# Decay scans that read PSUM and restart by a maximum, in an RWKV-6 plus mixture-of-depths kernel

## The chip, the cores and the metric

The kernel runs on one core of a Trainium2 chip. The metric is the device time of one execution in microseconds (us); the lower, the better. The engines of the core are TensorE (PE, with its weight loads PEld), VectorE (DVE), ScalarE (ACT), GpSimd (POOL) and SyncE (SP), which here only issues DMAs. PE writes its results to PSUM, and the other memory that the engines read is SBUF.

## What is computed

The first block is a linear attention with a decay per channel, over batch B = 4, heads H = 8, sequence S = 768 and head size D = 48:

```python
for t in range(S):
    cur = einsum('bhd,bhe->bhde', u * k_t, v_t)
    y[:, :, t] = einsum('bhd,bhde->bhe', r_t, state + cur)
    state = w_t[..., None] * state + einsum('bhd,bhe->bhde', k_t, v_t)
```

The second block takes y as rows of 384 = H * D numbers. It scores each row with a vector, picks the 128 best rows of each batch, sends them through a two-layer MLP (384 to 1024, ReLU, back to 384) and adds the result, gated by a sigmoid of the score, to these rows. All is float32. The decays w lie between 0.8 and 0.95.

## The kernel before, in words

**Tiling.** The sequence of a batch is cut into 6 chunks of L = 128 steps, 24 chunks in all. Two heads are one pair, each head padded to 64 channels, so a pair fills 128 partitions; HP = 4 pairs lie side by side, 128 steps each (W = 512 columns).

**Work on a chunk.** `decays` (lines 203 to 236) transposes the chunk's decays on PE (line 200, four transposes into one PSUM buffer `ps_t`), copies them with ACT into the SBUF buffer `wz` with a zero column between two pairs (line 208), and makes two running products with DVE scans over all four pairs at once. `right` (line 211) runs backward and holds, for each step, the product of the decays behind it. A scan step is state = data0 * state + data1; the zero column clears the state and `from_right` adds a 1 there, so each pair begins anew. The full product of a chunk, `all`, is a column of `right`; its reciprocal (line 218) is the start value, in `from_left`, of the forward scan `left` (line 223). Two ACT activations then check that the decays are in range (line 232). `scaled` (line 238) transposes k and r on PE and multiplies them by `right` and `left` (line 244, DVE): tiles K and R. `own` (line 247) makes the term with u, two products and one more on POOL (lines 251, 252, 256) with a DVE sum between (line 254), and issues the loads of a later chunk on SP. `scores` (line 260) multiplies K by R on PE and masks the result on DVE (line 271, `sc`). `back` (line 274) transposes K on PE, and ACT copies it out of PSUM (line 277, `kt`). `outputs` (line 282) sums the state part (line 289) and the chunk's own part (line 295) on PE; DVE adds (line 300, `x`) and scores the rows (line 302). `carry` (line 309) brings the state on: PE (line 319), DVE (lines 327 or 330), POOL (line 328, times the next chunk's `all`), ACT (line 334, into `s_buf`).

**Buffers.** The transposes of w, k, r and K share one pool of three PSUM buffers (`psT`, line 93, tag "t"). A buffer is given back when the last reader of its tile has ended.

**Order.** The loop from line 491 writes the pieces in this order for chunk n: scores(n), own(n+1), scaled(n+1), back(n), outputs(n), decays(n+2), carry(n), with one step of the previous batch's `mixture` between two pieces. The order on each engine is set when the program is built: a list scheduler goes by this order as priority and by its own estimates of when an instruction is ready, and so lets a later piece's instruction fill the time in which an earlier one waits. On the chip each engine then runs its list in order. After the last chunk `mixture` of the last batch runs by itself.

Of the kernel before, what the change touches and what calls it, by code (L numbers as in the profile page):

```python
# [10 lines left out]
FP32 = mybir.dt.float32  # L11
# [4 lines left out]
ALU = mybir.AluOpType  # L16
AX = mybir.AxisListType

L = 128
# [18 lines left out]
def kernel(  # L38
# [28 lines left out]

    nc = tc.nc  # L70
    PSUM = bass.MemoryType.PSUM

    B, H, S, D = r.shape
# [4 lines left out]
    HP = H // 2  # L78
# [1 line left out]
    NFC = F // L  # L80
    NHF = NCH // 2
    W = HP * L
    LS = L + 1
    WS = HP * LS
    assert S % (2 * L) == 0 and C % L == 0 and F % (4 * L) == 0 and H % 2 == 0
    assert D <= DP and W <= 512 and C <= 512 and 0 < CAP < S and CAP % L != 1
    assert B * NCH < 256
# [82 lines left out]
    nc.vector.tensor_copy(out=ids, in_=number)  # L170


    from_right = consts.tile([L, WS], FP32)
    nc.any.memset(from_right, 0.0)
    nc.vector.memset(from_right.rearrange("p (j t) -> p j t", t=LS)[:, :, 0], 1.0)
    from_left = [consts.tile([L, WS], FP32, name=f"from_left{i}") for i in range(2)]
    for t in from_left:
        nc.any.memset(t, 0.0)

    wz_bufs = [consts.tile([L, WS + 1], FP32, name=f"wz_buf{i}") for i in range(2)]  # L180
    for t in wz_bufs:
        nc.any.memset(t, 0.0)

    s_bufs = [consts.tile([L, HP, 2, D], FP32, name=f"s_buf{i}") for i in range(2)]
    for t in s_bufs:
# [2 lines left out]
    views = dram_disjoint_views(out, B)  # L188
    score = consts.tile([L, B, NCH], FP32)
    guard = consts.tile([L, N, 2], FP32)  # L190

    def by_pair(ap, at):

        return ap[:, at:at + WS].rearrange("p (j t) -> p j t", t=LS)[:, :, 0:L]


    def transposed(src, j=None):
# [5 lines left out]
    def decays(t):  # L203
        n = t["n"]
        wb = w_bufs[n % NBUF]
        ps = transposed(lambda j: wb[:, 2 * j:2 * j + 2, :])
        wz = wz_bufs[n % len(wz_bufs)]
        nc.scalar.copy(out=by_pair(wz, 1), in_=ps)  # L208
        yield
        right = lev.tile([L, WS + 4], FP32, tag="right", name="right", bufs=3)  # L210
        nc.vector.tensor_tensor_scan(  # L211
            out=right[:, WS:0:-1], data0=wz[:, WS:0:-1], data1=from_right, initial=0.0,
            op0=ALU.mult, op1=ALU.add,
        )
        t["right"] = right
        t["all"] = right[:, 1:1 + WS].rearrange("p (j t) -> p j t", t=LS)[:, :, 0]
        start = from_left[n % len(from_left)]
        nc.vector.reciprocal(  # L218
            out=start.rearrange("p (j t) -> p j t", t=LS)[:, :, 0], in_=t["all"]
        )  # L220
        yield
        left = lev.tile([L, WS], FP32, tag="left", name="left")
        nc.vector.tensor_tensor_scan(  # L223
            out=left, data0=wz[:, 0:WS], data1=start, initial=0.0,
            op0=ALU.mult, op1=ALU.add,
        )
        t["left"] = left
        yield

        junk = lev.tile([L, H, D], FP32, tag="junk", name="junk")  # L230
        for i, (bias, scale) in enumerate(((low, -1.0), (high, 1.0))):
            nc.scalar.activation(
                out=junk, in_=wb[:, :, 0:D], func=AF.Relu, bias=bias, scale=scale,
                accum_out=guard[:, n, i:i + 1],
            )
        yield

    def scaled(t):
        n = t["n"]
        rb, kb = r_bufs[n % NBUF], k_bufs[n % NBUF]  # L240
        for name, src, by in (("K", kb, by_pair(t["right"], 2)), ("R", rb, by_pair(t["left"], 0))):
            ps = transposed(lambda j: src[:, 2 * j:2 * j + 2, :])
            t[name] = lev.tile([L, HP, L], FP32, tag=name, name=name)
            nc.vector.tensor_mul(t[name], ps, by)  # L244
            yield
# [94 lines left out]
    def mixture(b):  # L340
# [38 lines left out]
        for gi, (c0, n) in enumerate(groups):  # L379

            pick = mod.tile([L, NCH, L], BF16, name="pick")
            at = rank
# [8 lines left out]
            for c in range(NCH):  # L391
# [2 lines left out]
                )  # L394
            idx = mod.tile([L, 1], UINT32, name="idx", bufs=2)
            nc.vector.tensor_scalar(
                out=idx, in0=ps[:, 0:1], scalar1=ps[:, 1:2], scalar2=None, op0=ALU.add
            )
            rows = views[b][0:b + 1].rearrange("b s c -> (b s) c")
            where = bass.IndirectOffsetOnAxis(ap=idx[0:n, 0:1], axis=0)  # L400
# [188 lines left out]
```

## Time and profile before

| what | value |
|---|---|
| time, median of 3 runs | 338.93 us (337.67 to 341.52) |
| the profiled execution's own time | 339.1 us |
| its span in the profile | 337.3 us |
| busy: PE, DVE, POOL, ACT | 272.4, 207.9, 111.6, 85.5 us |
| mean granted PE clock | 0.77 of full speed |
| instructions | 5344 |

The span runs from the first to the last instruction that the profile shows; 1.8 us of the execution's time lie around it. Busy times of different engines overlap, so they are not added up. A line number is that of the kernel before.

### The profile page before, as it was taken

How to read it: one execution, taken by the hardware profiler on the slowest of the kernel's cores; microseconds unless marked ns; L12 is line 12 of the kernel's file. 1: busy time of each engine (PE TensorE's matmuls, PEld its weight loads, DVE VectorE, ACT ScalarE, POOL GpSimd, SP SyncE). 2: the span in 40 equal slices, each digit the busy share in tenths (PEclk: the TensorE clock that was granted, in tenths of full speed). 3: DMA queues.
4: the chain of work that ended last, by engine and by line, in shares of the span. 5: the costliest groups of instructions: out<-in, count | busy, mean ns of one | idle time of the engine just before them, and what ended most of it. 6: DMA issues, size and time to landing. Idle time of an engine off the chain costs nothing.

```text
span 337.3 us, 5344 instructions
## 1 busy us (share of the span) xinstructions
PE 272.4 (81%) x2034; PEld 239.5 (71%) x2034; DVE 207.9 (62%) x411; ACT 85.5 (25%) x209; POOL 111.6 (33%) x108
## 2 busy tenths in 40 slices
PE   0148797997979899979869899979879899992691
PEld 0037796996967798769768699678867699681570
DVE  6139777677986854785976753866986723737100
ACT  1143334143431412331520402332411103120010
POOL 2154446364700664254600343264600200010001
PEclk9999859587875569995965559996965559995597
DMA  7999767355867811462633501464400000010001
GB/s 251 258 200 172 126 117 119 77 98 84 139 98 122 113 48 36 107 141 69 133 57 72 117 23 25 93 151 87 96 2 23 23 25 0 25 48 23 26 0 33
DMA packets 105570, 29.14 MB, mean 86 GB/s; under 512 B 100416, under 2 KB 104768, under 8 KB 105536
## 3 DMA queue, kind: packets, MB, share of 16 engines
q1 hardware_dynamic: 103584, 23.99, 40.4%
q10 hardware_dynamic: 1440, 3.15, 2.6%
q0 software_dynamic: 512, 1.57, 1.6%
q8 instruction: 18, 0.29, 0.4%
q14 instruction: 16, 0.13, 0.2%
HBM read 23.20 MB, written 5.51 MB: 85 GB/s over the span
## 4 chain that ended last, share of the span: by engine, by line
PE 58%; DVE 17%; DMA 7%; issue 7%; SPq 5%; POOL 3%; ACT 1%; POOLq 0%; DVEq 0%; ACTq 0%
PE ps_y L295 15%; PE ps_h L444 9%; PE ps_t L200 9%; PE ps_y L289 7%; PE ps_s L265 6%; PE ps_f L455 6%; DVE left L223 4%; DVE right L211 4%; PE ps_kv L319 3%; DMA xe<-out_dram,idx 3%; DMA r_buf<-in_r_dram 2%; DVE ahead L361 2%; DVE scr L302 2%; SPq L121 2%; DVE sc L271 1%
## 5 line engine op out<-in xcount | busy, mean ns | idle before, releaser
L295 PE MATMUL ps_y<-v,sc 128*128 128x48 f32 x384 | 71.0, 318 | 7.6 <-DVE sc L271 7.6
L295 PEld LDWEIGHTS ps_y<-v,sc 128*128 128x128 f32 x384 | 67.7, 248 | 9.2 <-DVE sc L271 8.7
L289 PE MATMUL ps_y<-s_buf,R 128*128 128x96 f32 x160 | 42.5, 357 | 10.4 <-ACT s_buf L334 10.4
L300 DVE TENSOR_TENSOR x<-ps_y,vo 128x384 f32<-128x384 f32 x24 | 13.4, 558 | 60.3 <-PE ps_y L295 60.3
L256 POOL TENSOR_TENSOR vo<-v,own 128x384 f32<-128x384 f32 x24 | 26.5, 1106 | 71.6 <-DVE x L300 36.2
L265 PE MATMUL ps_s<-R,K 48*128 48x128 f32 x384 | 42.4, 354 | 0.0
L289 PEld LDWEIGHTS ps_y<-s_buf,R 128*128 128x128 f32 x160 | 32.3, 250 | 11.8 <-ACT s_buf L334 11.8
L211 DVE TENSOR_TENSOR_SCAN right<-wz_buf,from_right 128x516 f32<-128x516 f32 x24 | 36.9, 1536 | 5.9 <-ACT wz_buf L208 5.9
L265 PEld LDWEIGHTS ps_s<-R,K 48*128 48x128 f32 x384 | 34.2, 242 | 5.9 <-issue 3.0
L200 PE MATMUL ps_t<-ident,w_buf 128*128 128x128 f32 x96 | 21.0, 354 | 19.5 <-DMA w_buf<-in_w_dram 16.2
L251 POOL TENSOR_TENSOR rk<-r_buf,k_buf 128x384 f32<-128x384 f32 x24 | 29.5, 1231 | 20.0 <-DMA r_buf<-in_r_dram 20.0
L252 POOL TENSOR_TENSOR rk<-rk,u_bc 128x384 f32<-128x384 f32 x24 | 34.0, 1421 | 1.8 <-DMA u_bc<-in_u_dram 0.5
L328 POOL TENSOR_TENSOR state<-mid,right 128x192 f32<-128x192 f32 x16 | 12.2, 763 | 66.1 <-DVE from_left L218 41.1
L444 PE MATMUL ps_h<-xeT,w 128*128 128x128 f32 x192 | 32.5, 346 | 0.6 <-ACT xeT L414 0.6
L223 DVE TENSOR_TENSOR_SCAN left<-wz_buf,from_left 128x516 f32<-128x516 f32 x24 | 32.3, 1345 | 0.2
L444 PEld LDWEIGHTS ps_h<-xeT,w 128*128 128x128 f32 x192 | 31.4, 259 | 1.3 <-ACT xeT L414 1.0
L271 DVE TENSOR_TENSOR sc<-ps_s,before_f 128x512 f32<-128x512 f32 x48 | 30.9, 675 | 1.7 <-PE ps_s L265 1.5
L200 PEld LDWEIGHTS ps_t<-ident,w_buf 128*128 128x128 f32 x96 | 15.5, 198 | 21.6 <-issue 16.5
L208 ACT COPY wz_buf<-ps_t 128x512 f32<-128x512 f32 x24 | 14.1, 585 | 59.3 <-PE ps_t L200 58.8
L277 ACT COPY kt<-ps_t 128x512 f32<-128x512 f32 x24 | 13.9, 581 | 50.3 <-PE ps_t L200 50.1
L200 PE MATMUL ps_t<-ident,r_buf 128*128 128x128 f32 x96 | 20.8, 355 | 6.6 <-DVE K L244 6.6
L334 ACT COPY s_buf<-state 64x192 f32<-64x192 f32 x40 | 14.0, 350 | 40.0 <-POOL state L328 34.7
(83 smaller groups left out, 352.6 us busy)
## 6 DMA issues: line engine op xcount, KB each, us to landing
w_buf<-in_w_dram SPq DMA_DIRECT2D x24, 192.0 KB, 3.2
k_buf<-in_k_dram SPq DMA_DIRECT2D x24, 192.0 KB, 4.0
r_buf<-in_r_dram SPq DMA_DIRECT2D x24, 192.0 KB, 4.5
v<-in_v_dram SPq DMA_DIRECT2D x24, 192.0 KB, 3.5
out_dram<-x SPq DMA_DIRECT2D x24, 192.0 KB, 2.0
w<-in_moe_w_dram ACTq DMA_DIRECT2D x2, 1536.0 KB, 9.8
u_bc<-in_u_dram SPq DMA_DIRECT2D x1, 192.0 KB, 4.3
wg_bc<-in_moe_w_gate_dram SPq DMA_DIRECT2D x1, 192.0 KB
```

What stands on the lines that cost most here:

```text
L200: nc.tensor.transpose(ps[:, j, :], src(j), ident)
L211: nc.vector.tensor_tensor_scan(out=right[:, WS:0:-1], data0=wz[:, WS:0:-1], data1=from_right, initial=0.0, op0=ALU.mult, op1=ALU.add,)
L223: nc.vector.tensor_tensor_scan(out=left, data0=wz[:, 0:WS], data1=start, initial=0.0, op0=ALU.mult, op1=ALU.add,)
L251: nc.gpsimd.tensor_mul(rk, rb[:, :, 0:D], kb[:, :, 0:D])
L252: nc.gpsimd.tensor_mul(rk, rk, u_bc)
L256: nc.gpsimd.tensor_mul(t["vo"], values[n], o.to_broadcast([L, H, D]))
L265: nc.tensor.matmul(ps[:, par, j, :], t["K"][rows, j, :], t["R"][rows, j, :], start=True, stop=True,)
L271: nc.vector.tensor_mul(t["sc"][:, par], ps[:, par], _heads(before_f, HP))
L289: nc.tensor.matmul(y[:, 2 * j:2 * j + 2, :], t["R"][:, j, :], s_bufs[n % len(s_bufs)][:, j], start=True, stop=False,)
L295: nc.tensor.matmul(y[:, h, :], t["sc"][:, par, j, :], vt[:, h, :], start=(ci == 0), stop=(ci == 0 or par == 1),)
L444: nc.tensor.matmul(ps[:, q, :], w1[:, dc, (f0 + q) * L:(f0 + q + 1) * L], xeT[:, dc, :], start=(dc == 0), stop=(dc == NDC - 1),)
L455: nc.tensor.matmul(ps, hid[:, fc, :], w2[:, fc, :], start=(fc == 0), stop=(fc == NFC - 1))
```

## The change

The ACT copy to `wz` and the zero columns go. Both scans read the transposed decays where PE left them, in PSUM, 511 columns instead of 516. The restart between two pairs is made by a maximum in place of the sum: a step is now state = max(data0 * state, data1), with data1 zero but at a pair's first step, where it holds 1 (backward) or the reciprocal of `all` (forward); the product that runs on from the pair before is never above these. `right` is written so that the last column of the last pair is a constant 1, set once in three fixed buffers. `all` is now its own tile of 128x4, a DVE product of a column of PSUM and a column of `right`. The first column of `left` is copied by ACT, one element per partition, since the forward scan writes from the second column on. K and R read `right` and `left` without gaps. In `mixture`, the sum that makes the row index takes a maximum with the batch's first row in the same instruction.

```diff
-    from_right = consts.tile([L, WS], FP32)
+    from_right = consts.tile([L, HP, L], FP32)
...
-    wz_bufs = [consts.tile([L, WS + 1], FP32, name=f"wz_buf{i}") for i in range(2)]
-    for t in wz_bufs:
-        nc.any.memset(t, 0.0)
+    right_bufs = [consts.tile([L, HP, L], FP32, name=f"right_buf{i}") for i in range(3)]
+    for t in right_bufs:
+        nc.vector.memset(t[:, HP - 1, L - 1:L], 1.0)
...
         ps = transposed(lambda j: wb[:, 2 * j:2 * j + 2, :])
-        wz = wz_bufs[n % len(wz_bufs)]
-        nc.scalar.copy(out=by_pair(wz, 1), in_=ps)
-        yield
-        right = lev.tile([L, WS + 4], FP32, tag="right", name="right", bufs=3)
+        wt = ps.rearrange("p j t -> p (j t)")
+
+        right = t["right"] = right_bufs[n % len(right_bufs)]
+        flat = right.rearrange("p j t -> p (j t)")
         nc.vector.tensor_tensor_scan(
-            out=right[:, WS:0:-1], data0=wz[:, WS:0:-1], data1=from_right, initial=0.0,
-            op0=ALU.mult, op1=ALU.add,
+            out=flat[:, W - 2::-1], data0=wt[:, W - 1:0:-1],
+            data1=from_right.rearrange("p j t -> p (j t)")[:, W - 2::-1], initial=1.0,
+            op0=ALU.mult, op1=ALU.max,
         )
-        t["right"] = right
-        t["all"] = right[:, 1:1 + WS].rearrange("p (j t) -> p j t", t=LS)[:, :, 0]
+        t["all"] = lev.tile([L, HP], FP32, tag="all", name="all", bufs=3)
+        nc.vector.tensor_mul(t["all"], ps[:, :, 0], right[:, :, 0])
         start = from_left[n % len(from_left)]
-        nc.vector.reciprocal(
-            out=start.rearrange("p (j t) -> p j t", t=LS)[:, :, 0], in_=t["all"]
+        nc.vector.reciprocal(out=start[:, :, 0], in_=t["all"])
+        yield
+
+        left = t["left"] = lev.tile([L, HP, L], FP32, tag="left", name="left")
+        nc.scalar.copy(out=left[:, 0, 0:1], in_=start[:, 0, 0:1])
+        nc.vector.tensor_tensor_scan(
+            out=left.rearrange("p j t -> p (j t)")[:, 1:W], data0=wt[:, 0:W - 1],
+            data1=start.rearrange("p j t -> p (j t)")[:, 1:W], initial=start[:, 0, 0:1],
+            op0=ALU.mult, op1=ALU.max,
         )
-        yield
-        left = lev.tile([L, WS], FP32, tag="left", name="left")
-        nc.vector.tensor_tensor_scan(
-            out=left, data0=wz[:, 0:WS], data1=start, initial=0.0,
-            op0=ALU.mult, op1=ALU.add,
-        )
-        t["left"] = left
...
             nc.vector.tensor_scalar(
-                out=idx, in0=ps[:, 0:1], scalar1=ps[:, 1:2], scalar2=None, op0=ALU.add
+                out=idx, in0=ps[:, 0:1], scalar1=ps[:, 1:2], scalar2=float(b * S),
+                op0=ALU.add, op1=ALU.max,
             )
```

## Rows read from the trace of the kernel before

**Rows 1.** Page: busy time by engine; granted PE clock in 40 slices.

```profile
PE 272.4 (81%) x2034; PEld 239.5 (71%) x2034; DVE 207.9 (62%) x411; ACT 85.5 (25%) x209; POOL 111.6 (33%) x108
...
PEclk9999859587875569995965559996965559995597
```

**Rows 2.** Windows of 2 us: width, busy per engine, PEclk, DMA share, GB/s.

```profile
76.00:78.00 2.00, 0.01 (x1) 0.00 (x0) 2.00 (x3) 1.18 (x3) 1.92 (x2) 1.00 1.44 185
...
80.00:82.00 2.00, 2.00 (x11) 2.00 (x11) 0.31 (x1) 0.00 (x0) 0.00 (x0) 0.50 0.00 0
```

**Rows 3.** Chain that ended last, shares of the span by line.

```profile
PE ps_y L295 15%; PE ps_h L444 9%; PE ps_t L200 9%; PE ps_y L289 7%; PE ps_s L265 6%; PE ps_f L455 6%; DVE left L223 4%; DVE right L211 4%; PE ps_kv L319 3%; DMA xe<-out_dram,idx 3%; DMA r_buf<-in_r_dram 2%; DVE ahead L361 2%; DVE scr L302 2%; SPq L121 2%; DVE sc L271 1%
```

**Rows 4.** The same chain in order of time: start, us, what.

```profile
22.61 1.45 DVE left L223
24.06 1.71 DVE right L211
...
242.48 1.94 DVE right L211
...
246.24 1.14 DVE left L223
```

**Rows 5.** Single lines' instructions: duration ns min/median/max, first and last start.

```profile
L211 DVE TENSOR_TENSOR_SCAN right<-wz_buf,from_right x24: 1220/1429/2243, 10.8 to 286.7; 128x516 f32<-128x516 f32 x24
...
L223 DVE TENSOR_TENSOR_SCAN left<-wz_buf,from_left x24: 1214/1223/1850, 22.5 to 288.2; 128x516 f32<-128x516 f32 x24
...
L271 DVE TENSOR_TENSOR sc<-ps_s,before_f x48: 656/680/692, 30.3 to 299.5; 128x512 f32<-128x512 f32 x48
...
L252 POOL TENSOR_TENSOR rk<-rk,u_bc x24: 993/1402/1922, 21.0 to 243.4; 128x384 f32<-128x384 f32 x24
...
L300 DVE TENSOR_TENSOR x<-ps_y,vo x24: 556/558/558, 34.7 to 303.3; 128x384 f32<-128x384 f32 x24
...
L302 DVE CUSTOM_DVE_ANT_0 scr<-x,wg_bc x24: 534/556/1353, 35.7 to 303.9; 128x384 f32<-128x384 f32 x24
```

**Rows 6.** Groups by line: busy us, mean ns of one, idle before and releaser.

```profile
L208 ACT COPY wz_buf<-ps_t 128x512 f32<-128x512 f32 x24 | 14.1, 585 | 59.3 <-PE ps_t L200 58.8 <-ACT s_buf L334 0.5
...
L218 DVE RECIPROCAL from_left<-right 128x4 f32<-128x4 f32 x24 | 4.1, 172 | 0.2
...
L428 ACT ACTIVATE neg<-neg 128x1 f32<-128x1 f32 x4 | 0.8, 202 | 0.7 <-DVE neg L425 0.6
```

**Rows 7.** Timeline of one chunk: start, us, engine, line, work, [idle before].

```profile
74.06 1.53 DVE L211 TENSOR_TENSOR_SCAN right<-wz_buf,from_right 128x516 f32<-128x516 f32 x1
...
75.21 0.60 PE L200 MATMUL ps_t<-ident,K 128*128 128x128 f32 x4
...
75.62 0.18 DVE L218 RECIPROCAL from_left<-right 128x4 f32<-128x4 f32 x1
...
75.84 1.63 DVE L223 TENSOR_TENSOR_SCAN left<-wz_buf,from_left 128x516 f32<-128x516 f32 x1
...
77.40 1.25 DVE L271 TENSOR_TENSOR sc<-ps_s,before_f 128x512 f32<-128x512 f32 x2
78.11 0.30 PEld L295 LDWEIGHTS ps_y<-v,sc 128*128 128x128 f32 x2 [2.27 <-DVE sc L271]
...
79.18 0.67 DVE L244 TENSOR_TENSOR R<-ps_t,left 128x512 f32<-128x512 f32 x1
```

**Rows 8.** Waits, whole span: us in total, times, longest us.

```profile
DVE own L254 <- POOL rk L252: 12.9, 5, 9.8
...
DVE right L211 <- ACT wz_buf L208: 5.9, 6, 3.8
...
PEld ps_t L200 <- ACT wz_buf L208: 2.4, 3, 1.1
```

**Rows 9.** Timeline of a chunk with mixture work, PE weight loads and DVE.

```profile
111.13 0.71 PEld L200 LDWEIGHTS ps_t<-ident,k_buf 128*128 128x128 f32 x4 [0.64 <-ACT wz_buf L208]
...
111.81 0.68 DVE L244 TENSOR_TENSOR K<-ps_t,right 128x512 f32<-128x512 f32 x1
```

More of the change, by code (lines that the diff above doesn't have):

```diff
@@ L82 @@
     W = HP * L
-    LS = L + 1
-    WS = HP * LS
     assert S % (2 * L) == 0 and C % L == 0 and F % (4 * L) == 0 and H % 2 == 0
@@ L170 @@
     nc.vector.tensor_copy(out=ids, in_=number)
-    from_right = consts.tile([L, WS], FP32)
+    from_right = consts.tile([L, HP, L], FP32)
     nc.any.memset(from_right, 0.0)
-    nc.vector.memset(from_right.rearrange("p (j t) -> p j t", t=LS)[:, :, 0], 1.0)
-    from_left = [consts.tile([L, WS], FP32, name=f"from_left{i}") for i in range(2)]
+    nc.vector.memset(from_right[:, :, L - 1], 1.0)
+    from_left = [consts.tile([L, HP, L], FP32, name=f"from_left{i}") for i in range(2)]
     for t in from_left:
         nc.any.memset(t, 0.0)
-    wz_bufs = [consts.tile([L, WS + 1], FP32, name=f"wz_buf{i}") for i in range(2)]
-    for t in wz_bufs:
-        nc.any.memset(t, 0.0)
+    right_bufs = [consts.tile([L, HP, L], FP32, name=f"right_buf{i}") for i in range(3)]
+    for t in right_bufs:
+        nc.vector.memset(t[:, HP - 1, L - 1:L], 1.0)
     s_bufs = [consts.tile([L, HP, 2, D], FP32, name=f"s_buf{i}") for i in range(2)]
@@ L190 @@
     guard = consts.tile([L, N, 2], FP32)
-    def by_pair(ap, at):
-        return ap[:, at:at + WS].rearrange("p (j t) -> p j t", t=LS)[:, :, 0:L]
     def transposed(src, j=None):
@@ L206, in decays @@
         ps = transposed(lambda j: wb[:, 2 * j:2 * j + 2, :])
-        wz = wz_bufs[n % len(wz_bufs)]
-        nc.scalar.copy(out=by_pair(wz, 1), in_=ps)
+        wt = ps.rearrange("p j t -> p (j t)")
[5 more added lines that the diff above has]
+            op0=ALU.mult, op1=ALU.max,
+        )
+        t["all"] = lev.tile([L, HP], FP32, tag="all", name="all", bufs=3)
+        nc.vector.tensor_mul(t["all"], ps[:, :, 0], right[:, :, 0])
+        start = from_left[n % len(from_left)]
+        nc.vector.reciprocal(out=start[:, :, 0], in_=t["all"])
         yield
-        right = lev.tile([L, WS + 4], FP32, tag="right", name="right", bufs=3)
+        left = t["left"] = lev.tile([L, HP, L], FP32, tag="left", name="left")
+        nc.scalar.copy(out=left[:, 0, 0:1], in_=start[:, 0, 0:1])
         nc.vector.tensor_tensor_scan(
-            out=right[:, WS:0:-1], data0=wz[:, WS:0:-1], data1=from_right, initial=0.0,
-            op0=ALU.mult, op1=ALU.add,
-        )
-        t["right"] = right
-        t["all"] = right[:, 1:1 + WS].rearrange("p (j t) -> p j t", t=LS)[:, :, 0]
-        start = from_left[n % len(from_left)]
-        nc.vector.reciprocal(
-            out=start.rearrange("p (j t) -> p j t", t=LS)[:, :, 0], in_=t["all"]
-        )
-        yield
-        left = lev.tile([L, WS], FP32, tag="left", name="left")
-        nc.vector.tensor_tensor_scan(
-            out=left, data0=wz[:, 0:WS], data1=start, initial=0.0,
-            op0=ALU.mult, op1=ALU.add,
-        )
-        t["left"] = left
+            out=left.rearrange("p j t -> p (j t)")[:, 1:W], data0=wt[:, 0:W - 1],
+            data1=start.rearrange("p j t -> p (j t)")[:, 1:W], initial=start[:, 0, 0:1],
+            op0=ALU.mult, op1=ALU.max,
+        )
         yield
@@ L240, in scaled @@
         rb, kb = r_bufs[n % NBUF], k_bufs[n % NBUF]
-        for name, src, by in (("K", kb, by_pair(t["right"], 2)), ("R", rb, by_pair(t["left"], 0))):
+        for name, src, by in (("K", kb, t["right"]), ("R", rb, t["left"])):
             ps = transposed(lambda j: src[:, 2 * j:2 * j + 2, :])
```

## The prediction

> **What bounds the kernel now.** I read the page's busy times first. PE is the busiest engine, 272.4 of 337.3 us, DVE has 207.9 and ACT 85.5 [rows 1]. [...] The 2 us windows show what goes before a fall: from 76 to 78 us PE is all but idle (0.01 us) while DVE is busy without a gap, and by 80 to 82 us the clock is at half and PE full [rows 2]. So the loop alternates: at full clock DVE holds PE up, at half clock PE bounds and DVE has time to spare. A faster DVE pays only in the first kind of stretch.
>
> The chain's shares show the same: PE lines lead, yet each of the two scans holds 4% of the span [rows 3], together 0.08 x 337.3 = 27.0 us. In order of time this is 19 pieces, 9 of `right` and 10 of `left`; the first and last of each are shown, and they run from 1.14 to 1.94 us [rows 4]. That spread is the point. The single lines say why: scans take 1.22 us at best, but `right` has a median of 1.43 and a worst of 2.24 us [rows 5]. `sc`, whose one operand is in PSUM, stays within 656 to 692 ns in all 48 instances, and `x`, also from PSUM, within 556 to 558. `scr`, which reads two SBUF tiles as the scans do, goes from 534 to 1353 ns. POOL's product L252 goes from 993 to 1922 ns [rows 5]. I conclude that a DVE instruction with two SBUF tensors and a POOL instruction hold each other up when they meet, and that one with an operand in PSUM doesn't. The slowest `right` of the chunk shown, 1.53 us from 74.06, is such a case [rows 7].
>
> **The change part by part.** Sums are made against the profiled execution, 339.1 us (span 337.3, with 1.8 around it); the median shown is 338.93, so 0.2 lower.
>
> *Scans from PSUM.* With one SBUF tensor left, the scans should stop stretching. On the chain a scan that isn't stretched takes 1.14 us from its start to the next [rows 4]; 19 x 1.14 = 21.7 against 27.0, so -5.3. Five columns fewer of 516 are 1%, nothing. Bounds: the trace has no scan from PSUM. The nearest rows are `x` (one operand in PSUM, 558 ns) and `scr` (both in SBUF, 556 ns), the same 384 columns [rows 5]: no difference. If the stretching stayed the gain would be 0; if a backward walk through PSUM cost a scan what the worst stretching costs now (1.85 for 1.22 us [rows 5], +0.63), 19 x 0.63 = +12 on top of -5.3. I take -5.3, because both PSUM rows are flat. [...]
>
> *The product `all`.* 24 more small DVE instructions, each between `right` and the reciprocal and dependent on both sides. The nearest row is the reciprocal itself, 128x4 in 172 ns [rows 6], and in the chunk shown 0.04 us lies between it and `left` [rows 7]; so 0.2 us where right and left lie on the chain together, about 9 chunks: +1.8. Bounds: 0 where another instruction fills the gap, 24 x 0.21 = +5 if all count.
>
> *The ACT copy goes.* 24 x 585 ns leave ACT [rows 6], which is a quarter busy, so the busy time itself is worth nothing. What counts is that `right` no longer waits for it: DVE waited 5.9 us, of which 3.8 once, at the start, where the next DVE work stands behind loads anyway [rows 8]. Of the 2.1 left I take half as on the chain, -1.1 (bounds 0 and -2.1): `right` is then late for what DVE has before it.
>
> *POOL runs freer.* L252 stretches to twice its best under a scan [rows 5], and DVE's sum `own` waits for it: 12.9 us, 9.8 of them at the start behind loads, 3.1 in four others [rows 8]. Unstretched, L252 ends up to 0.9 us sooner. I take -1.4, under half of 3.1, since `right` must end too (bounds 0 and -3.1).
>
> *The PSUM buffer is held longer.* This is what the change gives back. Before, the buffer of w's transposes came free when ACT's copy ended, 585 ns after the transposes. Now it stays taken through `right`, `all`, the reciprocal and `left`. There are three, and the next two go to k and r, whose multiplications (line 244) stand behind `left` on DVE. So K's transposes of `back` find none until `left` ends. In the chunk shown they ran at 75.21, while `left` ran from 75.84 to 77.47 [rows 7]: they would start with `left`'s end. PE stood still then anyway, 2.27 us until `sc` [rows 7], and `sc` needs 0.6 us more; the transposes (0.60) fit beside it, and only the state matmuls queued behind them on PE come late, some 0.3 us. With six such chunks at full clock: +1.8. In chunks with mixture work the pool is short already: three times PE's loads waited for ACT's copy to give the buffer back [rows 8], once for k at 111.13. There the next buffer would come free with the K multiplication, 111.81 + 0.68 = 112.5 [rows 9], 1.4 us later; I count half of it, as PE has other waits close by: 3 x 0.7 = +2.1. Bounds for the part: 0 where the builder puts other PE work first, and 24 x 0.6 + 3 x 1.4 = +19 if every chunk paid its transposes in full.
>
> *The rest.* The new ACT copy of one element is at most 202 ns, the price of the 128x1 activation [rows 6]. It is covered by `left`: it can start with the reciprocal's end, 75.80 in the chunk shown, and R's multiplication, its only reader, starts at 79.18 [rows 7]. If ACT had a wait in front of it that cover could go; 24 x 0.2 = +5 is its bound. Memsets at the start lie before the first decays arrive. The maximum in the index adds no instruction, and no DMA is added or moved on any queue.
>
> Sum: -5.3 + 1.8 - 1.1 - 1.4 + 1.8 + 2.1 = -2.1, so 339.1 - 2.1 = **337.0 us**, no change that a measurement could tell: about 1% (3.4 us) is what this kernel's runs can tell from none.
>
> **The rivals.**
>
> *The waits of PE get short enough to keep the clock (faster).* `right`, `all`, reciprocal and `left` form a longer row of dependent instructions, and the builder fills such gaps with ready work: `sc` may come ahead of `left`. PE's 2.27 us wait [rows 7] would lose up to the 1.63 us of `left`, and the fall to half clock that follows it [rows 2] could fail to come. For: it is always a wait on DVE that goes before. Against: at half clock the loop gains nothing. Some five chunks at 1.5 us: -7.5; five more chunks then run at full clock and pay the 0.3 us of late state matmuls, +1.5. So 337.0 - 7.5 + 1.5 = 331.0.
>
> *The held buffer becomes the bound (slower).* One mechanism: K's transposes wait for `left`, `kt` for them, so `carry` and the next chunk's state come late, and PE's wait grows instead of shrinking. It decides once the transposes cost more than the 0.6 us of `sc` beside which I hid them: at half clock they take longer, and the DVE list may put other work between `right` and `left`. At 0.6 us more in 15 chunks, +9: 346. [...] Against: half the chunks are PE bound, where `left` ends before PE gets to these transposes.
>
> *The scans don't get faster.* If reading PSUM backward, or the maximum, costs what the stretching cost, term one is gone: 337.0 + 5.3 = 342.3, and up to 349 at the bound. For it speaks only that no such row exists; against it the flat PSUM rows.
>
> **How the numbers follow.** My forecast has 0.46, the clock rival 0.27, the held buffer 0.17, the slow scans 0.10. The forecast's own range is 333 to 341: a tenth of it lies below 335.5. Faster by over 1%: 0.05 of the forecast, 0.26 of the clock rival and 0.01 of the slow scans, 0.32. Slower by over 1% (above 342.5): most of the held buffer and half of the slow scans, 0.16 + 0.06 = 0.22. Within 1%: 0.46. The range goes from the middle of the first rival's gain to the middle of the second's loss, 329 to 345, and leaves out what lies beyond at either end, about 2 in 10.
>
> **What would show it.** Right: in the profile after, both scans are near 1.2 us with little spread, L252 and the other POOL products go down in their mean, ACT loses 14 us, and the chain's scan shares fall to about 3% each. K's transposes should start with `left`'s end at full clock. Wrong: scans with a mean above 1.4 us; `sc` ahead of `left` and fewer falls of the clock (the first rival); PE loads of `ps_t` that wait for `left` by more than 10 us in all (the second); R's multiplication waiting for ACT.

## The result and the profile after

The changed kernel takes 317.64 us (median of 4 runs, 316.48 to 318.77), the kernel before 340.23 us (4 runs, 337.67 to 342.52) beside it: a ratio of 0.934, 95% interval 0.925 to 0.942. That is 22.6 us faster, ten times the 2.1 us forecast and outside the range of 329 to 345. The profiled execution took 316.48 us, its span is 314.7 us. The ratios with an interval, here and below, leave out runs that are more than 1.5% above the fastest of their kernel; where a kernel's runs scatter more widely, the median over all of them is given too.

The page of the kernel after, busy times and granted PE clock in 40 slices:

```profile
PE 250.9 (80%) x2034; PEld 220.4 (70%) x2034; DVE 201.6 (64%) x436; ACT 76.3 (24%) x209; POOL 89.0 (28%) x108
...
PEclk9999999769955579995955879995855899995597
```

This pair of lines, against [rows 1], carries the result. PE runs the same 2034 instructions, but is busy 250.9 us with them instead of 272.4: 21.5 us less. The rest of the span, in which PE does nothing, went from 337.3 - 272.4 = 64.9 to 314.7 - 250.9 = 63.8 us: 1.1 us less. In the sum the change took hardly any waiting from PE; its instructions ran at the higher clock for longer (mean granted clock 0.82 of full speed, 0.77 before). By the trace's clock records, which read either full speed or half of it, PE stands at half for 155 us of the span before and 113 us after. The records begin at 32.0 us before and at 24.7 us after, and the page counts what lies ahead of the first one as full clock. The number of falls is nearly the same, ten before and nine after: the low stretches got shorter.

Single lines of the kernel after (duration ns min/median/max): the two scans and POOL's second product.

```profile
L207 DVE TENSOR_TENSOR_SCAN right_buf<-ps_t,from_right x24: 1208/1210/1222, 10.3 to 264.3; 128x511 f32<-128x511 f32 x24
...
L220 DVE TENSOR_TENSOR_SCAN left<-ps_t,from_left x24: 1261/1271/1281, 20.0 to 266.3; 128x511 f32<-128x511 f32 x24
...
L249 POOL TENSOR_TENSOR rk<-rk,u_bc x24: 992/1002/1312, 21.3 to 227.8; 128x384 f32<-128x384 f32 x24
```

The stretching of [rows 5] is gone, on both sides: no scan is more than 20 ns from its best, and POOL's product has a median of 1002 instead of 1402 ns.

Groups of the kernel after (busy us, mean ns of one, idle before): the two new instructions.

```profile
L219 ACT COPY left<-from_left 128x1 f32<-128x1 f32 x24 | 4.6, 191 | 72.0 <-DVE from_left L215 71.9
L213 DVE TENSOR_TENSOR all<-ps_t,right_buf 128x4 f32<-128x4 f32 x24 | 3.7, 152 | 0.0
```

Waits of the kernel after (us in total, times, longest us):

```profile
DVE right_buf L207 <- PE ps_t L196: 11.9, 4, 6.9
...
PE ps_t L196 <- DVE left L220: 6.4, 9, 1.9
```

The second line is the held PSUM buffer. PE's waits for `sc` and for the K multiplication, 7.6 and 6.6 us in all before, are no longer in the list; those for `s_buf` went from 10.4 to 13.0 us.

Where the time goes shows best in the start of each chunk's `x`. The first comes at 34.72 us before and at 29.29 after (5.4 us won); chunk 3 at 62.89 and 52.15 (10.7); chunk 12, behind the first batch's `mixture`, at 163.89 and 152.80 (11.1); chunk 15 at 210.34 and 194.30 (16.0); chunk 21 at 285.57 and 263.81 (21.8). So there are four steps of about 5 us each: the start, chunks 1 to 3, and the `mixture` stretches of the second and the third batch. They are steps of one execution of each kernel. In e10 below, as fast as the kernel after, chunk 3 comes 4.0 us later, at 56.18, and chunk 12 at 152.52 us: what is lost in one stretch can come back in another.

In chunks 1 to 3 the step is the clock. Before, it falls at 38.8 us, behind this wait of PE, and stays low until 49.1; after, it doesn't fall until 58.8.

```profile
38.68 0.56 PE L295 MATMUL ps_y<-v,sc 128*128 128x48 f32 x2 [1.76 <-DVE sc L271]
```

**The start.** DVE in the kernel before, then in the kernel after (start us, us, engine, line, work, idle before):

```profile
12.07 0.18 DVE L218 RECIPROCAL from_left<-right 128x4 f32<-128x4 f32 x1
22.06 0.55 DVE L254 TENSOR_REDUCE own<-rk 128x8 f32<-128x384 f32 x1 [9.81 <-POOL rk L252]
22.53 1.53 DVE L223 TENSOR_TENSOR_SCAN left<-wz_buf,from_left 128x516 f32<-128x516 f32 x1
23.99 1.79 DVE L211 TENSOR_TENSOR_SCAN right<-wz_buf,from_right 128x516 f32<-128x516 f32 x1
```

```profile
11.53 0.16 DVE L213 TENSOR_TENSOR all<-ps_t,right_buf 128x4 f32<-128x4 f32 x1
18.62 1.22 DVE L207 TENSOR_TENSOR_SCAN right_buf<-ps_t,from_right 128x511 f32<-128x511 f32 x1 [6.92 <-PE ps_t L196]
19.76 0.15 DVE L215 RECIPROCAL from_left<-all 128x4 f32<-128x4 f32 x1
19.88 0.16 DVE L213 TENSOR_TENSOR all<-ps_t,right_buf 128x4 f32<-128x4 f32 x1
19.95 1.27 DVE L220 TENSOR_TENSOR_SCAN left<-ps_t,from_left 128x511 f32<-128x511 f32 x1
```

Before, `own` of chunk 0 stands ahead of both scans in DVE's list and waits until 22.06 us for POOL, which waits for the load of u. After, the list scheduler has other dependences to go by and puts `own` behind the scans, which are done by 23 us. The order isn't all of the 5.4 us: in the runs below that keep this order of the start, the first `x` comes between 29.35 and 33.77 us, and the clock has a part in that. After, the first clock record, at the full level, begins at 24.7 us; in e14 PE's transposes still take over 1 us at 27 us, the record begins at 37.2, and the first `x` comes at 33.04.

**The mixture stretch of the second batch.** PE in the kernel before, then in the kernel after, at the same place of the program:

```profile
186.60 1.12 PE L200 MATMUL ps_t<-ident,w_buf 128*128 128x128 f32 x4 [0.68 <-ACT kt L277]
...
188.40 1.12 PE L200 MATMUL ps_t<-ident,k_buf 128*128 128x128 f32 x4 [0.54 <-ACT wz_buf L208]
```

```profile
174.06 1.02 PE L196 MATMUL ps_t<-ident,K 128*128 128x128 f32 x4 [0.17 <-DVE left L220]
...
175.76 0.66 PE L196 MATMUL ps_t<-ident,w_buf 128*128 128x128 f32 x4 [0.55 <-ACT kt L274]
176.26 0.60 PE L196 MATMUL ps_t<-ident,k_buf 128*128 128x128 f32 x4
```

Four transposes take 1.12 us at half clock and 0.60 to 0.66 at full clock: after, the clock is back up at 174.9 us, before it stays down until 202.7. One wait differs. Before, k's transposes are put into the PSUM buffer that ACT's copy of the decays gives back, and stand 0.54 us behind w's transposes for it. After, that buffer is held by the scans, k's transposes get another one that is free by then, and follow at once. But that is not what brought the clock back here, for it was up before PE got to w's and k's transposes (windows of the kernel after: width, busy and instructions of PE, PEld, DVE, ACT, POOL, then PEclk, DMA share, GB/s):

```profile
174.00:174.80 0.80, 0.74 (x4) 0.71 (x4) 0.80 (x2) 0.00 (x0) 0.00 (x0) 0.50 0.72 140
174.90:175.70 0.80, 0.31 (x8) 0.22 (x6) 0.80 (x3) 0.58 (x1) 0.00 (x0) 1.00 0.83 158
```

What did bring it back is not shown; e9 and e13 below come back to it.

### The profile page after: what moved, and what is told of

Its sections match the earlier page's. It is cut to its first block, busy times and chain, and to the rows that moved or that the text cites. A ratio compares the mean times of both kernels' runs of the same rounds, so it can differ in the third digit from the quotient of the medians.

```text
span 314.7 us, 5360 instructions
## 1 busy us (share of the span) xinstructions
PE 250.9 (80%) x2034; PEld 220.4 (70%) x2034; DVE 201.6 (64%) x436; ACT 76.3 (24%) x209; POOL 89.0 (28%) x108
## 4 chain that ended last, share of the span: by engine, by line
PE 57%; DVE 15%; DMA 10%; issue 8%; SPq 3%; ACT 2%; POOL 2%; POOLq 0%; DVEq 0%; ACTq 0%
PE ps_y L292 14%; PE ps_t L196 11%; PE ps_h L442 8%; PE ps_y L286 8%; PE ps_f L453 7%; PE ps_s L262 4%; DMA xe<-out_dram,idx 4%; DMA w_buf<-in_w_dram 4%; DVE right_buf L207 4%; DVE ahead L358 3%; DVE left L220 2%; PE ps_kv L316 2%; DVE scr L299 2%; DVE x L297 2%; SPq L122 2%
## 5 line engine op out<-in xcount | busy, mean ns | idle before, releaser
L292 PE MATMUL ps_y<-v,sc 128*128 128x48 f32 x384 | 65.6, 300 | 0.6 <-ACT left L219 0.6
L292 PEld LDWEIGHTS ps_y<-v,sc 128*128 128x128 f32 x384 | 62.8, 232 | 1.3 <-ACT left L219 0.7
L207 DVE TENSOR_TENSOR_SCAN right_buf<-ps_t,from_right 128x511 f32<-128x511 f32 x24 | 29.1, 1212 | 12.0 <-PE ps_t L196 11.9
L253 POOL TENSOR_TENSOR vo<-v,own 128x384 f32<-128x384 f32 x24 | 21.6, 900 | 44.0 <-DVE x L297 29.3
L248 POOL TENSOR_TENSOR rk<-r_buf,k_buf 128x384 f32<-128x384 f32 x24 | 24.7, 1029 | 31.2 <-DMA r_buf<-in_r_dram 31.2
L325 POOL TENSOR_TENSOR state<-mid,all 128x192 f32<-128x192 f32 x16 | 8.3, 516 | 80.1 <-DVE all L213 40.4
L220 DVE TENSOR_TENSOR_SCAN left<-ps_t,from_left 128x511 f32<-128x511 f32 x24 | 30.5, 1271 | 0.1
L442 PEld LDWEIGHTS ps_h<-xeT,w 128*128 128x128 f32 x192 | 26.2, 220 | 1.3 <-ACT xeT L412 1.0
L249 POOL TENSOR_TENSOR rk<-rk,u_bc 128x384 f32<-128x384 f32 x24 | 25.0, 1045 | 2.0 <-DMA u_bc<-in_u_dram 0.5
L196 PE MATMUL ps_t<-ident,K 128*128 128x128 f32 x96 | 18.9, 332 | 6.5 <-DVE left L220 6.4
L453 PE MATMUL ps_f<-w,hid 128*128 128x384 f32 x64 | 23.4, 496 | 0.0
```

Source lines behind the costliest of these rows:

```text
L196: nc.tensor.transpose(ps[:, j, :], src(j), ident)
L207: nc.vector.tensor_tensor_scan(out=flat[:, W - 2::-1], data0=wt[:, W - 1:0:-1], data1=from_right.rearrange("p j t -> p (j t)")[:, W - 2::- ...
L220: nc.vector.tensor_tensor_scan(out=left.rearrange("p j t -> p (j t)")[:, 1:W], data0=wt[:, 0:W - 1], data1=start.rearrange("p j t -> p (j ...
L248: nc.gpsimd.tensor_mul(rk, rb[:, :, 0:D], kb[:, :, 0:D])
L249: nc.gpsimd.tensor_mul(rk, rk, u_bc)
L253: nc.gpsimd.tensor_mul(t["vo"], values[n], o.to_broadcast([L, H, D]))
```

## The experiments

"In the lists of after" means that on PE, DVE, ACT and POOL each instruction is chained to the one before it in the order of the kernel after; so the work changes and the order doesn't. For the kernel after with an edit, "in its own lists" means the same, but for e6, where only DVE and POOL are chained. `x` numbers count from 0. The table has the profiled execution of each run: its span, PE's busy time and the rest of the span, the first `x`, and two steps in which the clock can come back, from `x` 13 to 14 and from 19 to 20.

| run | span | PE busy | PE idle | first x | 13 to 14 | 19 to 20 |
|---|---|---|---|---|---|---|
| before | 337.3 | 272.4 | 64.9 | 34.72 | 18.68 | 18.25 |
| after | 314.7 | 250.9 | 63.8 | 29.29 | 16.34 | 15.12 |
| e1 | 337.2 | 274.9 | 62.3 | 33.77 | 18.73 | 18.77 |
| e2 | 337.4 | 267.9 | 69.5 | 35.05 | 16.98 | 16.99 |
| e3 | 330.9 | 266.7 | 64.2 | 32.72 | 18.57 | 18.23 |
| e4 | 335.4 | 272.7 | 62.7 | 37.64 | 16.17 | 18.85 |
| e5 | 319.4 | 255.3 | 64.1 | 30.10 | 16.16 | 15.10 |
| e6 | 323.3 | 261.6 | 61.7 | 36.09 | 15.86 | 15.15 |
| e7 | 315.0 | 257.6 | 57.4 | 31.84 | 18.73 | 18.77 |
| e8 | 307.8 | 254.6 | 53.2 | 29.45 | 18.18 | 15.50 |
| e9 | 332.4 | 266.8 | 65.6 | 30.57 | 16.30 | 18.18 |
| e10 | 314.5 | 251.5 | 63.0 | 29.94 | 16.37 | 15.09 |
| e11 | 315.9 | 256.8 | 59.1 | 32.28 | 18.18 | 18.18 |
| e12 | 316.9 | 258.6 | 58.3 | 30.63 | 18.18 | 18.18 |
| e13 | 318.8 | 253.4 | 65.4 | 32.01 | 18.19 | 18.19 |
| e14 | 317.0 | 253.3 | 63.7 | 33.04 | 15.93 | 15.21 |
| e15 | 325.1 | 264.4 | 60.7 | 30.12 | 15.91 | 15.77 |
| e16 | 317.1 | 258.8 | 58.3 | 33.37 | 18.19 | 15.52 |
| e17 | 304.7 | 249.7 | 55.0 | 29.35 | 18.19 | 15.78 |

Where POOL does its products, PE's idle time lies between 60.7 and 65.6 us, but for e2 (69.5) and for e11 and e12, which give PE extra work in an idle stretch. Among these, spans that are 22 us apart differ by PE's busy time. Where POOL's products are gone (e7, e8, e16, e17), the idle time is 53.2 to 58.3 us: there part of the gain is waiting, and not clock.

**e1 and e2: the order alone, the new instructions alone.** Two theories: A, the gain is the order of the lists; B, it is the speed of the new instructions. e1 is the work of before in the lists of after, e2 the work of after with DVE and POOL in the order of before.

```diff
+    for before, after in zip(order, order[1:]):
+        tc.add_manual_dep(mine[after], mine[before].name, ...)
```

> The kernel before (ACT copy, scans from SBUF, zero columns), but with the instructions of PE, DVE, ACT and POOL held in the order that the changed kernel's lists have; the copy itself is free in its place. Theory A (order: the new dependences made the builder write better lists, and these carry the gain): 318 to 324 us, first x at 29 to 30 us. Theory B (speed: scans that don't stretch and a copy less carry the gain): 334 to 341, with stretched scans (mean above 1.4 us for right).

> The changed kernel, but DVE and POOL held in the order that the lists of the kernel before have, with `all` anywhere between (PE and ACT are left to the builder, since PE's old list needs PSUM buffers that are now held longer). Theory A (order): 334 to 341 us, first x at 33 to 35. Theory B (speed): 316 to 322, first x at 29 to 31. If both hold in part: 322 to 334, and the first x tells how much of the start is order.

e1: 336.27 us against 338.84, ratio 0.994 (0.989 to 0.998). e2: 339.88, ratio 1.003 (0.999 to 1.008). Neither has the gain. By e1 the order alone isn't it. e2 is not a clean test in the mixture stretches, where the old order clashes with the held buffer (PE idle 69.5): it says that the new work doesn't help in those lists of DVE and POOL, and not what it is worth in lists that suit it. With POOL's products in place, the gain was seen only where work and lists go together.

**e3 and e6: the order of the start.** e3 is the kernel before with `own` of chunk 0 written behind `scaled` of chunk 0; e6 the kernel after with DVE's first instructions in the order of before, `own` of chunk 0 ahead of the first `left` again; the scheduler, left free on PE and ACT, changed those lists too.

```diff
-    piece(own, 0)
...
+    piece(own, 0)
```

> The kernel before with one line moved at the start: own(0) is traced behind scaled(0) instead of in front of decays(1), so that DVE's first left no longer stands behind the sum that waits for the load of u. Theory A: the start alone gives 4 to 6 us, so 333 to 336, first x at 29 to 31 instead of 34.7. Theory B: first x within 1 us of 34.7 and 338 to 341.

> The kernel after, in its own lists but for DVE's first 14 instructions, which stand in the order of before: own of chunk 0 (it waits for a load of u) ahead of left of chunk 0. If the 5.4 us won before the first output come from this order, the first x starts at 33 to 35 us instead of 29.3 and the whole costs 322 to 325. If the order matters only together with the short scans, and the clock that is up by 25 us carries on into chunks 1 to 3, the loss is larger, 326 to 330. If the start is won back later by itself: 318.

e3: 332.06 against 338.84, ratio 0.980 (0.974 to 0.987). e6: 324.40 against 338.21, ratio 0.953 (0.941 to 0.964), where the kernel after has 0.934. The order of the start is worth about 2% in either kernel, 6 to 7 us, with what the scheduler rearranged for it in the other lists. e6's first `x` comes at 36.09; the wait is the old one again (waits, e6):

```profile
DVE own L259 <- POOL rk L257: 11.3, 1, 11.3
```

**e4: the copy back.** The kernel after with ACT's copy to SBUF, and scans that read it, in the lists that the scheduler then makes.

```diff
-        wt = ps.rearrange("p j t -> p (j t)")
+        wz = lev.tile([L, HP, L], FP32, tag="wz", name="wz_buf")
+        nc.scalar.copy(out=wz, in_=ps)
+        wt = wz.rearrange("p j t -> p (j t)")
```

> The changed kernel (restart by maximum, `all` as a tile, no gaps) with ACT's copy put back and both scans and `all` reading the SBUF copy, so PSUM is given back early and scans can stretch again. Its DVE list has the first left behind own(0) as before and differs in the loop. Theory A: about 322 to 328, by its lists, scans stretched or not. Theory B: 334 to 342, right's mean at 1.45 to 1.6 us.

Median 337.43 against 338.84, no difference that these runs, from 331.85 to 340.33, can tell. So the maximum, `all` as its own tile and the gapless K and R bring nothing that can be told by themselves: the gain hangs on reading PSUM, with what that does to the lists, the buffer and ACT's hop.

**e5 and e14: are the scans' microseconds the gain?** e5 has a DVE memset of 0.33 us behind each `right`, e14 one of 0.23 us and a POOL memset of 0.48 us behind each product with u.

```diff
+        pad = lev.tile([L, 205], FP32, tag="pad", name="pad", bufs=1)
+        nc.vector.memset(pad, 0.0)
...
+        slow = lev.tile([L, 460], FP32, tag="slow", name="slow", bufs=1)
+        nc.gpsimd.memset(slow, 0.0)
```

> The kernel after, with every engine's list held in its own order, and behind each of the 24 right scans a DVE memset of 128x330 (about 0.33 us), which puts back about what a right scan was longer before (1.43 to 1.21 us in the median). Theory T (threshold: the gain goes through PE's granted clock, which is kept only while PE's waits on DVE are short): much of the gain goes, far more than the scans' own time on the chain; 24 x 0.33 = 7.9 us is all that the memsets last, and only about half stand on a chain, so 4 us would be the direct price; by T the loss is 8 to 16 us, about 326 to 334, with 20 us more of half clock. Theory D (direct: each stretched scan costs what it lasts): 320 to 324.

> The kernel after in its own lists, with a DVE memset of 128x205 (about 0.25 us) behind each right scan and a POOL memset of 128x460 (about 0.5 us) behind each product with u: about the lengths that the stretching added before (right 1.43 against 1.21 us; POOL's three products 0.1, 0.3 and 0.15 us more), without a hop. If the stretched instructions carry the 16 us: 326 to 334. If not: 318 to 322, as with the dose on right alone (320.5).

e5: 320.47, ratio 0.942 (0.932 to 0.953). e14: 320.30 against 342.66 on its chip, 0.935 by the medians. Groups of e14:

```profile
L215 DVE TENSOR_TENSOR_SCAN right_buf<-ps_t,from_right 128x511 f32<-128x511 f32 x24 | 29.1, 1214 | 12.7 <-PE ps_t L204 12.7
...
L261 POOL MEMSET slow<- 128x460 f32 x24 | 11.5, 481 | 0.0
...
L221 DVE MEMSET pad<- 128x205 f32 x24 | 5.5, 229 | 0.0
```

5.5 us more on DVE and 11.5 on POOL, laid evenly behind the instructions that had been stretched, cost nothing that can be measured in the whole; the mixture steps stay at 15.93 and 15.21. In e14's profiled run `x` is 3.8 us late in chunk 0 and 7.9 in chunk 3, but only 2.0 in chunk 12: a loss at the start was made up again. The 0.8% of e5, 2.8 us, can't be told from nothing either (0.932 to 0.953 against 0.925 to 0.942); in its profiled run `x` is 0.8 us late in chunk 0, 4.2 in chunk 3 and 4.7 in the last. I had expected 8 to 16 us of e5 from a threshold of the clock, a guess of mine that no trace shows, and that fell too: evenly longer DVE work lost no clock that shows in the whole.

**e9: the PSUM buffer held, nothing else.** The work of before in the lists of after, as e1, but DVE reads one column of the transposed decays behind `left`, into a tile that nothing reads. The buffer is so held as long as in the kernel after.

```diff
+        last = lev.tile([L, 1], FP32, tag="last", name="last")
+        nc.vector.tensor_copy(out=last, in_=ps[:, 0, 0:1])
```

> The work of before (ACT copy, scans from SBUF) in the lists of after, and behind each left scan a DVE copy of one column of the transposed decays, 128x1, that nothing reads: the PSUM buffer of the decays is now held until left has ended, as in after. Theory P (the buffer given back early is what harms: k's transposes are put into the buffer that ACT's copy frees and wait 0.5 to 0.7 us for it in the mixture stretches of batches 2 and 3, just when PE could get its clock back): those waits go, steps 14 and 20 fall from 18.7 to about 16 us, and the whole is 5 to 10 us below the same lists without the hold (336.3): 326 to 331. Prediction on record (the hold costs): 337 to 341. If neither: 336 to 337.

Ratio 0.976 (0.969 to 0.983), where e1 has 0.994 (0.989 to 0.998). But that ratio rests on e9's three fastest runs; its ten scatter from 327.56 to 341.97, and their median is 334.25 against 337.96, or 0.989, where e1's median gives 0.992. So a gain from holding the buffer, of 0.3 to 1.8%, is not shown; nor is any cost. PE of e9 at the place shown above, then PE of e1 and of e13 (described below):

```profile
184.27 1.09 PE L208 MATMUL ps_t<-ident,K 128*128 128x128 f32 x4 [0.17 <-DVE last L236]
185.15 0.34 PE L402 MATMUL ps_i<-ids,pick 128*128 128x2 bf16 x6
186.04 1.12 PE L208 MATMUL ps_t<-ident,w_buf 128*128 128x128 f32 x4 [0.54 <-ACT kt L287]
186.94 1.06 PE L208 MATMUL ps_t<-ident,k_buf 128*128 128x128 f32 x4
```

```profile
184.91 1.12 PE L208 MATMUL ps_t<-ident,w_buf 128*128 128x128 f32 x4 [0.33 <-ACT kt L285]
186.71 1.12 PE L208 MATMUL ps_t<-ident,k_buf 128*128 128x128 f32 x4 [0.68 <-ACT wz_buf L216]
```

```profile
173.07 1.09 PE L204 MATMUL ps_t<-ident,K 128*128 128x128 f32 x4 [0.17 <-DVE left L230]
...
174.84 1.12 PE L204 MATMUL ps_t<-ident,w_buf 128*128 128x128 f32 x4 [0.54 <-ACT kt L284]
175.75 1.06 PE L204 MATMUL ps_t<-ident,k_buf 128*128 128x128 f32 x4
```

The wait for ACT's copy is gone in e9, the clock comes back at 190.3 us, behind k's transposes, and step 13 to 14 falls from 18.73 to 16.30. Step 19 to 20 falls only to 18.18. With the wait for the copy (before, e1, e3, e4, and e7 below) one of 10 such steps is under 17 us; without it (after and the 12 runs from e5 on but e7) 16 of 26, and the two of e2 (16.98 and 16.99). That goes with theory P but doesn't show it. In 10 of the 16 the clock is up before w's and k's transposes, as in the kernel after, so that the absent wait can't be the reason. And e13 has the same PE work as e9 and the kernel after from 5 us before `x` 13 to w's transposes 9 us behind it, with the same waits of 0.17 and 0.54 us; yet the clock comes back 7.8 us behind `x` 13 in the kernel after, 13.0 in e9 and 21.0 in e13. So neither that wait nor PE's work in these microseconds settles by itself whether the clock comes back, and what does stays open.

**e13 and e15: ACT's hop.** An ACT pass over the transposed decays writes ones, and `right` takes its start value from there: the hop and its hand-over are back, the scans still read PSUM. e15 has the doses of e14 as well.

```diff
+        one = lev.tile([L, HP, L], FP32, tag="one", name="one")
+        nc.scalar.activation(out=one, in_=ps, func=AF.Copy, bias=1.0, scale=0.0)
...
-            ... initial=1.0,
+            ... initial=one[:, 0, 0:1],
```

> The kernel after in its own lists, with an ACT pass of 128x512 between the transposes and the right scan (it writes ones from the transposed decays times 0, and the scan takes its start value 1 from there): the hop of before is back, about 0.6 us and a hand-over before each right scan, but the scans read PSUM and nothing stretches. If the hop carries the 16 us: 328 to 334. If the stretching does: 318 to 321.

> Both together: the hop over ACT and the doses on DVE and POOL. If these are what separates the two kernels in the same lists: 330 to 336, by as much above the two single runs as a clock that gives way to the sum would make it. If something else is at work: below 326.

e13: 322.47 against 342.66, ratio 0.943 (0.933 to 0.953). e15: 325.01, ratio 0.947 (0.938 to 0.957). The hop's 1% can't be told from nothing, and both together, 1.4%, are at the edge of what these runs can tell: 4 to 5 us of the 14 or more (0.976 less 0.934) that separate e9 from the kernel after.

**e7, e8, e16 and e17: POOL reads no SBUF.** POOL's three products are memsets, which leaves the u term out (short ones in e7 and e8, as long as unstretched products in e16 and e17); e7 and e16 have the work of before, e8 and e17 that of after, all in the lists of after, e16 also with the hold.

```diff
-        nc.gpsimd.tensor_mul(rk, rb[:, :, 0:D], kb[:, :, 0:D])
-        nc.gpsimd.tensor_mul(rk, rk, u_bc)
+        nc.gpsimd.memset(wide, 0.0)
+        nc.gpsimd.memset(wide, 0.0)
```

> The work of before in the lists of after, with POOL's three own-term products replaced by POOL memsets, so that the u term is left out and POOL reads no SBUF while the scans run; the ACT copy to SBUF and its hop stay. If the stretching by POOL is what the order alone lacked: scans near 1.22 us and 318 to 322. If it is ACT's hop and copy: 333 to 337, as with POOL's products. In between, each has a part.

> The work of after in its own lists, with the same POOL memsets in place of the three products (the u term left out). Its scans do not stretch anyway, so it stays at 316 to 318; the products themselves (1.03 us each) are shorter as memsets, so own may come up to 0.5 us sooner. Its distance to the same edit on the work of before is what ACT's hop and the held PSUM buffer are worth together.

> The work of before in the lists of after, the PSUM buffer held as in after, and POOL's three products of the own term replaced by POOL memsets that last as long as the unstretched products (128x945 and 128x830); the u term is left out, and POOL reads no SBUF in them. The ACT copy, its hop and the scans from SBUF stay. If the meeting of scans and POOL products carries the difference: scans at 1.22 to 1.25 us, and within 2 to 4 us (the hop) of the kernel after with the same memsets. If not: 10 us or more above it.

> The kernel after in its own lists with the same POOL memsets in place of the three products (the u term left out): the measure for the run before it. Its products had nothing to meet, so by that it stays near 316; POOL no longer waits for the loads of k, r and u or for own, which may bring up to 5 us.

e7: median 318.04 (307.08 to 324.79). e8: 307.87, ratio 0.902 (0.890 to 0.915). e16: 314.47, 0.923 (0.915 to 0.932). e17: 304.51, 0.887 (0.877 to 0.896). Single lines of e16 show the scans from SBUF unstretched:

```profile
L219 DVE TENSOR_TENSOR_SCAN right<-wz_buf,from_right x24: 1226/1233/1233, 10.9 to 267.4; 128x516 f32<-128x516 f32 x24
...
L231 DVE TENSOR_TENSOR_SCAN left<-wz_buf,from_left x24: 1215/1226/1311, 20.4 to 269.2; 128x516 f32<-128x516 f32 x24
```

So it is the meeting with POOL that stretches them: `right` takes up to 2243 ns where it reads SBUF beside POOL's products (before), at most 1233 where it reads SBUF and they are gone (e16), and 1208 to 1222 from PSUM beside them (after).

As a measure of the gain these runs are inconclusive. From e9 to e16 5.3% go, but from after to e17, where nothing met, 4.7% go too: POOL no longer waits for loads, and PE's idle time is 8.8 us less. And e16 lies 3.7% above e17, though in the main the hop is left between them, for which e13 shows 0.9%. (By the medians of all runs the three are 6.2, 3.6 and 2.9%.) The parts don't add up to one account; how the 9 us or more between e15 and e9 divide stays open. With the meeting of scans and POOL, the hop and the hold all in play, and each run's clock going one way or the other in a mixture stretch, the runs leave the sizes of the parts open.

**e10, e11, e12: can the start be better still?** e10 puts the reciprocal and `left` of chunk 0 directly behind its `right`; e11 gives PE 26 transposes of the identity, which nothing reads, while it waits for the second chunk's load; e12 does both.

```diff
+        if n == 0:
+            idle = psA.tile([L, L], FP32, tag="a", name="idle")
+            for _ in range(26):
+                nc.tensor.transpose(idle, ident, ident)
```

> The kernel after in its own lists, but with DVE's first 14 instructions in an order of our own: reciprocal and left of chunk 0 directly behind its right scan, ahead of right of chunk 1. left of chunk 0 then runs at 12 instead of 19.95 us, its PSUM buffer is free, and r's transposes (which waited until 21.33 for it) follow k's at 19.4: the first scores start about 2 us earlier. If the start is a plain chain and the clock follows as before: the first x at 26.5 to 27.5 instead of 29.3 us and the whole 314.5 to 316. If the clock falls earlier for it (PE has more to wait for afterwards): 317 to 321.

> The kernel after in its own lists, with 26 transposes of the identity on PE that nothing reads, between the transposes of the first and the second chunk's decays, where PE stands idle from 10.2 to 17.5 us. They end before 17.5 us (26 x 0.27 = 7.0 at half rate). If the granted clock is a matter of what PE did just before, the transposes from 17.5 us on take 0.60 instead of 1.08 us for four, the first x comes about 1 us earlier, and 316 to 317 in all; if the record of full clock in an idle stretch were right, nothing changes.

> Both edits: left of chunk 0 directly behind its right, and the 26 unread transposes on PE in the idle stretch. If both gains add: first x at 25 to 26 us, 313 to 315 in all, the fastest of the set. If the start is bound by loads (u_bc and the second chunk's k and r), the first x stays above 26.5 us and the second edit gives nothing.

e10: 315.10, ratio 0.928 (0.918 to 0.938). e11: 315.73, 0.932 (0.923 to 0.942). e12: 319.07, 0.943 (0.933 to 0.953). None can be told from the kernel after (0.925 to 0.942), though their first `x` lies at 29.94, 32.28 and 30.63 us. In e10 the scores start 1.9 us sooner (22.22 instead of 24.16 us), and the first `x` is no earlier: there the clock has fallen again at 28.0 us. In e11 the first `x` is 3 us late, and by chunk 12 the kernel is 3.9 us ahead (148.94 instead of 152.80). PE of e11:

```profile
10.07 4.68 PE L214 MATMUL idle<-ident 128*128 128x128 f32 x26
17.52 1.09 PE L204 MATMUL ps_t<-ident,w_buf 128*128 128x128 f32 x4 [2.78 <-DMA w_buf<-in_w_dram]
```

The first 16 of the 26 start 0.21 us apart, and the last 10, from 13.5 us on, 0.11 us apart; the trace's first clock record, at the full level, begins there too. After 2.78 us of idling four take 1.09 again; the records have the clock low from 16.9 to 30.6 us.

## Why the prediction was wrong, point by point

**What fails is the frame of the sum.** I wrote that a faster DVE "pays only in the first kind of stretch" and then priced each part in microseconds on the chain, against a trace whose clock stayed as it was. That the -2.1 us lie near the 1.1 by which PE's idle time shrank is luck, since several terms were wrong. The other 21.5 us are PE's own 2034 instructions, at the higher granted clock for longer, and the sum has no term for them. The first rival named the clock, at 331.0 and a chance of 0.27. Part of it came: PE's waits for `sc` are gone, and `sc` runs ahead of `left` in five chunks instead of two. But falls of the clock are hardly fewer, nine instead of ten; its price of -7.5 came from one kind of chunk (74 to 82 us) and left out the mixture stretches, where half of the gain lies and the low stretches got shorter. That "it is always a wait on DVE that goes before" a fall was a misreading: before five of the ten falls, PE's longest wait is for ACT's `s_buf` (0.9 to 3.6 us). Why the low stretches are shorter is the part that the runs leave open.

**Scans from PSUM, -5.3.** That they don't stretch is right, 1210 and 1271 ns in the median. That their own microseconds on the chain are the gain isn't borne out: e14 laid about as much back on DVE and POOL and lost nothing that can be told. The bound of +12 took 1.85 us as the worst stretching; `right` has 2.24 in [rows 5], so it should have been +19. PSUM as a source costs a scan nothing that shows: the same 511 columns take `right` 1.21 us at best from PSUM (after) and 1.21 from SBUF (e4), and `left` 1.26 and 1.27.

**The PSUM buffer held longer, +3.9.** No such cost shows. I read the three waits in [rows 8] as proof that the pool is tight and would be tighter. PE does wait 6.4 us for `left` now, but the waits for ACT's copy are gone: k's transposes had been given the buffer that was freed last. e9 holds the buffer alone and is 0.3 to 1.8% below e1, where +3.9 us would be 1.2% above it.

**The start, counted as nothing.** I set the 9.8 us of `own` and the 3.8 us of `right` aside as standing "behind loads". Only `own` stood behind that load; both scans stood behind `own`, in an order that the builder was free to change, and did. e3 and e6 price it at 6 to 7 us.

**The ACT copy, -1.1,** can't be checked: e13 shows about 1%, 3 us, for putting the hop back, which can't be told from nothing. **`all`, +1.8:** 152 ns each, and no row of its cost on the chain can be told. **The rest** was right: the one-element copy, 191 ns, is late for one PE load only. One small slip in the chances: half of the slow scans is 0.05, not 0.06.

**The second and third rivals** fell: PE's loads and transposes wait 6.4 us for `left`, not over 10, and no scan is slow.

## What to carry to other kernels

Before pricing an edit in microseconds on the chain, split the span into what PE is busy and what it is idle, and ask how much of its work runs at the lower clock: here two kernels that are 22 us apart have the same idle time to 1.1 us, and 17 us of added DVE and POOL work changed the whole by nothing that could be told. One profiled execution of each kernel doesn't say which edit brings a clock back: the same PE work, with the same waits, came out three ways. An edit that changes dependences also changes the lists of every engine; read the new order first, above all where a waiting instruction stands at the head of a list during the loads at the start. And a buffer that is given back early can be the wrong one to be given: PE then waited up to 0.7 us for it, three times in the run.

## What the runs showed of the hardware

- With PSUM as their source the scans were not stretched beside POOL's products, backward either: `right` 1208 to 1222 ns over all 24, and `left` 1261 to 1281. From SBUF `right` took 1220 to 2243 and `left` 1214 to 1850 (before).
- A start value read per partition cost `right` 67 ns: it has 1212 ns in the mean with the constant 1 and 1279 in e13 with the value from a tile, and nothing else changed in it. Group of e13:

```profile
L217 DVE TENSOR_TENSOR_SCAN right_buf<-ps_t,one,from_right 128x511 f32<-128x511 f32 x24 | 30.7, 1279 | 20.8 <-ACT one L212 20.8
```

- The page's clock reads full where the trace has no record yet. In the kernel after the first record begins at 24.7 us; the page reads full from the start, yet PE's four transposes take 1.06 to 1.12 us from 17.5 to 24 us. From 25.5 us on, where there is a record, they take 0.60 to 0.66, as it says. Ahead of the first record, durations of a known instruction tell the clock.
